# Seven products instead of eight in the second matmul of seven token tiles: operand sums on GpSimd, recombination on VectorE

## Chip, cores, metric

One core of one Trainium2 chip. The metric is the device time of one execution in microseconds (us); medians of several executions are given with their lowest and highest. Ratios are the mean time of one kernel's runs over the mean time of the other kernel's runs of the same rounds on the same chip, so they are not quite the ratio of the medians that are quoted beside them.

The engines' names in the profile are: PE = TensorE matmuls, PEld = TensorE weight loads, DVE = VectorE, ACT = ScalarE, POOL = GpSimd, SP = SyncE, SPq = the queue in which SyncE issues transfers. "L320" is line 320 of the kernel that was profiled. The changed kernel's first lines are one line longer, so L319 of the kernel before is L320 of the changed one. In an experiment, lines below an inserted edit move on: L395 of the changed kernel is L399 in e1 and L401 in e2.

## The reference

```python
# q, k, v: [8 batches, 8 heads, 576 positions, 64]
scores = (q @ k.T) / sqrt(64)
ret = scores * Dmat[head]             # causal decay mask gamma ** (i - j)
x = (ret @ v)                         # reordered to [4608 tokens, 512]
h = x @ w_in                          # 512 -> 2048
g = h * cos(h)
out = g @ w_out                       # 2048 -> 512, float32
```

The attention part is small. The two matmuls by `w_in` and `w_out` make most of the TensorE work.

## The kernel before

The kernel goes through the tokens in ten tiles, of 512, 256, 256 and then seven times 512 tokens; n counts them from 0, so "tile n=3" is the first of the last seven. For each tile it runs the first matmul (`mm1`, eight blocks of 1024 PSUM columns), takes the cosine on ScalarE, multiplies on VectorE into the bfloat16 tile `gT` (this multiplication is called the gate product below), and runs the second matmul (`mm2`). The attention work of the next tile's token groups (128 tokens each) is put between the matmuls of `mm2`, so that TensorE always has something to do:

```python
widths = [512, 256, 256] + [512] * 7
...
def mm1(n, et, c0, w, bank, inside={}):
    ...                                   # 8 matmuls 128x512 into one double bank: a, b or m
    nc.scalar.activation(cosh, ps, ACTF.Sin, bias=half_pi, scale=1.0)
    nc.vector.tensor_mul(gT[:, et : et + m, c0 : c0 + w], ps, cosh)

def mm2(n, tsi, et, c0=0, c1=DM):         # called 64 times in a tile of 512 tokens
    ...
    nc.tensor.matmul(ps, lhsT=gT[:, et, tsi * P : (tsi + 1) * P],
                     rhs=w_out_sb[:, et, c0:c1], start=(et == 0), stop=(et == ET - 1))
    if et == ET - 1:
        nc.scalar.copy(ot, ps)
        nc.sync.dma_start(out[...], ot)
        feed(s)                           # load, prepare and transpose later token groups
```

GpSimd prepares each token group. It scales q and k to bfloat16 and casts v (`prep`):

```python
nc.gpsimd.tensor_tensor(out=qks[:, 0], in0=fq, in1=tq, op=ALU.mult)
nc.gpsimd.tensor_tensor(out=qks[:, 1], in0=fk, in1=tk, op=ALU.mult)
nc.gpsimd.tensor_copy(vb, fv)
```

SyncE issues loads, stores and the transposes of `qks` in one queue, in program order, so a transpose that waits for GpSimd holds up the loads behind it. In the profile of the kernel before, transposes wait for GpSimd 15 times, 20.8 us in all, at most 2.7 us; one that begins at 66.13 us is released by GpSimd at 68.57 (3.46 us with its own issuing), and the load behind it begins at 69.63.

VectorE, besides `gT`, multiplies the masks into the scores (`ret`, out of PSUM banks a and b) and adds up the running attention states (`s`, out of bank st, then copied to bfloat16 `sb`). PSUM has double banks a, b and m, and single banks n and st.

## Time and profile before

In the rounds with the changed kernel, five executions had a median of 308.29 us (307.87 to 310.25). The first three of them alone had 310.21 us (308.17 to 310.25).

From the page of the kernel before: the span and the busy times, then three rows of the 40 equal slices of the span (a digit is the busy share in tenths), then the chain that ended last, by engine and by line (cut off at the end of the excerpt).

```profile
span 304.4 us, 5826 instructions
PE 295.5 (97%) x2411; PEld 169.2 (56%) x2441; DVE 172.9 (57%) x215; ACT 128.2 (42%) x145; POOL 101.1 (33%) x127
...
POOL 2780076445346355444536253415330000000000
PEclk9999999999999999999999999999999999999999
DMA  8999999999989999999999999389923600020012
...
PE 92%; DMA 5%; issue 1%; SPq 1%; DVE 0%; POOL 0%; ACT 0%; ACTq 0%
```

TensorE is the limit: it is busy for 97% of the span, is 92% of the chain, and its granted clock shows as 9 in every slice (0.999 in the mean). GpSimd is idle for two thirds, VectorE for over 40%. But the DMA row is full for the first 60% of the span: GpSimd is idle because it waits for loads. One line of the groups of instructions shows it (busy us and mean ns of one; then the idle time before them and what ended it):

```profile
L136 POOL TENSOR_TENSOR qks<-fq,gq 128x512 bf16<-128x512 f32 x32 | 33.3, 1042 | 98.0 <-DMA fq<-in_q_dram 95.4
```

I cut traces at the start of each tile's `mm1` and call the stretch from one start to the next the tile's period. Here are tiles n=2, 3 and 5 of the kernel before, with the busy times, the granted TensorE clock (PEclk), the busy share of the DMA engines and the rate:

```profile
core 0: us, PE busy (x) PEld busy (x) DVE busy (x) ACT busy (x) POOL busy (x), PEclk, DMA share, GB/s
67.50:83.94 16.44, 16.22 (x163) 11.19 (x165) 9.28 (x13) 6.54 (x7) 8.08 (x9) 1.00 1.21 206
83.94:117.04 33.10, 32.73 (x342) 23.22 (x344) 23.90 (x32) 14.20 (x15) 16.73 (x19) 1.00 1.08 213
...
148.83:180.19 31.36, 30.99 (x238) 15.74 (x240) 20.00 (x25) 13.27 (x14) 14.70 (x17) 1.00 1.23 221
```

TensorE is busy for 99% of each of these periods. This trace is of one of the kernel's quicker executions. A kernel with the same order of work (experiment e4) was traced at 308.46 us, with a span of 306.6 us. In it one transpose came late in tile n=2, TensorE waited 2.3 us for it, and the period was 18.7 instead of 16.4 us. So where the traces' spans are compared below, up to about 2 us in tile n=2 may be such a difference and not the change. The comparison of medians doesn't have this problem to the same degree.

### The profile page before, as it was taken

What the parts mean: (1) busy time and instruction counts of PE and PEld (TensorE: products, weight loads), DVE (VectorE), ACT (ScalarE), POOL (GpSimd) and SP (SyncE); (2) the same over time, 40 slices, a digit from 0 to 9 for tenths busy, and PEclk for the clock granted to TensorE, in tenths of its full rate; (3) what the DMA queues carried; (4) which work ended last, traced back from release to release, by engine and by line L of the source; (5) the groups of instructions that cost most, each with busy time, mean ns of one, the idle gap of its engine ahead of it and who ended that gap; (6) DMA issues with size and microseconds to landing.
All of it is one profiled execution on the core that took longest, in us unless ns stands there. A gap on an engine that the chain in (4) does not pass through costs nothing.

```text
span 304.4 us, 5826 instructions
## 1 busy us (share of the span) xinstructions
PE 295.5 (97%) x2411; PEld 169.2 (56%) x2441; DVE 172.9 (57%) x215; ACT 128.2 (42%) x145; POOL 101.1 (33%) x127
## 2 busy tenths in 40 slices
PE   8899999999999999999999999999999999999995
PEld 3578647758588554445544554455445544554444
DVE  5677514665687665774875566646765557504700
ACT  2656333515256224532364236422652255226511
POOL 2780076445346355444536253415330000000000
PEclk9999999999999999999999999999999999999999
DMA  8999999999989999999999999389923600020012
GB/s 208 202 209 207 208 219 194 220 228 203 209 181 207 220 216 248 228 221 195 223 242 223 187 263 196 49 196 210 254 35 86 89 34 2 34 71 34 0 71 69
DMA packets 150810, 50.19 MB, mean 165 GB/s; under 512 B 140800, under 2 KB 146304, under 8 KB 150784
## 3 DMA queue, kind: packets, MB, share of 16 engines
q1 hardware_dynamic: 146560, 45.63, 79.6%
q0 software_dynamic: 4224, 4.19, 8.4%
q8 instruction: 19, 0.31, 0.5%
q14 instruction: 7, 0.06, 0.1%
HBM read 36.70 MB, written 9.44 MB: 152 GB/s over the span
## 4 chain that ended last, share of the span: by engine, by line
PE 92%; DMA 5%; issue 1%; SPq 1%; DVE 0%; POOL 0%; ACT 0%; ACTq 0%
PE h L319 41%; PE o L336 40%; PE ov L292 3%; PE sc L179 3%; DMA w_in_sb<-in_moe_w_in_dram 2%; DMA fk<-in_k_dram 2%; PE ov L279 2%; PE st L238 1%; SPq L111 1%; PE st L208 0%; DVE xT L304 0%; POOL qks L137 0%; SPq L381 0%; PE tr L157 0%; ACT ot L345 0%
## 5 line engine op out<-in xcount | busy, mean ns | idle before, releaser
L336 PE MATMUL o<-w_out_sb,gT 128*128 128x512 bf16 (+2 forms) x586 | 126.2, 367 | 2.5 <-issue 2.2
L319 PE MATMUL h<-xT,w_in_sb 128*128 128x512 bf16 (+2 forms) x826 | 127.1, 313 | 0.7 <-DMA w_in_sb<-in_moe_w_in_dram 0.2
L328 DVE TENSOR_TENSOR gT<-h,cosh 128x1024 bf16<-128x1024 f32 x72 | 88.2, 1225 | 54.4 <-ACT cosh L327 54.3
L319 PEld LDWEIGHTS <-w_in_sb 128*128 128x128 bf16 x832 | 75.9, 98 | 50.4 <-issue 0.4
L327 ACT ACTIVATE cosh<-h,half_pi 128x1024 f32<-128x1024 f32 x72 | 80.2, 1113 | 51.3 <-PE h L319 51.3
L336 PEld LDWEIGHTS <-gT 128*128 128x128 bf16 x608 | 56.3, 98 | 62.0 <-issue 0.2
L136 POOL TENSOR_TENSOR qks<-fq,gq 128x512 bf16<-128x512 f32 x32 | 33.3, 1042 | 98.0 <-DMA fq<-in_q_dram 95.4
L345 ACT COPY ot<-o 128x512 f32<-128x512 f32 (+2 forms) x38 | 21.4, 563 | 86.4 <-PE o L336 86.3
L137 POOL TENSOR_TENSOR qks<-fk,gk 128x512 bf16<-128x512 f32 x35 | 36.5, 1043 | 16.2 <-DMA fk<-in_k_dram 14.4
L188 DVE TENSOR_TENSOR ret<-sc,tri 128x1024 bf16<-128x1024 f32 x32 | 38.0, 1218 | 4.1 <-PE sc L179 4.0
L304 ACT CAST xT<-ov 128x1024 bf16<-128x1024 f32 (+1 forms) x18 | 16.5, 917 | 21.4 <-PE ov L292 21.2
L143 POOL CAST vb<-fv 128x512 bf16<-128x512 f32 x32 | 19.6, 612 | 6.9 <-DMA fv<-in_v_dram 5.5
L261 DVE TENSOR_TENSOR s<-st,s 128x256 f32<-128x256 f32 x18 | 7.6, 424 | 24.3 <-PE st L238 24.0
L252 DVE CAST sb<-s 64x256 bf16<-64x256 f32 x48 | 19.2, 401 | 0.7
L292 PE MATMUL ov<-ret,vb 128*64 128x128 bf16 x288 | 12.0, 222 | 0.0
L217 DVE TENSOR_TENSOR sb<-st,diag 128x512 bf16<-128x512 f32 x8 | 5.5, 686 | 11.4 <-PE st L208 10.6
L259 DVE COPY s<-st 128x256 f32<-128x256 f32 x6 | 2.5, 424 | 15.8 <-PE st L238 15.8
L179 PEld LDWEIGHTS <-qkT 64*128 64x128 bf16 x288 | 8.1, 94 | 5.0 <-ACT qkT L162 2.3
L279 PEld LDWEIGHTS <-sb 128*128 128x128 bf16 x128 | 8.4, 98 | 3.8
L179 PE MATMUL sc<-qkT 64*128 64x128 bf16 x256 | 10.3, 217 | 0.0
L292 PEld LDWEIGHTS <-vb 128*64 128x64 bf16 x288 | 8.7, 109 | 2.0
L279 PE MATMUL ov<-qkT,sb 128*128 128x128 bf16 (+1 forms) x116 | 8.8, 215 | 0.1
(53 smaller groups left out, 76.3 us busy)
## 6 DMA issues: line engine op xcount, KB each, us to landing
out_dram<-ot SPq DMA_DIRECT2D x35, 256.0 KB, 4.2
fk<-in_k_dram SPq DMA_DIRECT2D x32, 256.0 KB, 4.8
fv<-in_v_dram SPq DMA_DIRECT2D x32, 256.0 KB, 5.0
fq<-in_q_dram SPq DMA_DIRECT2D x28, 256.0 KB, 4.1
w_in_sb<-in_moe_w_in_dram POOLq DMA_DIRECT2D x4, 512.0 KB, 8.6
w_out_sb<-in_moe_w_out_dram POOLq DMA_DIRECT2D x4, 512.0 KB, 15.9
fq<-in_q_dram SPq DMA_DIRECT2D x2, 512.0 KB, 4.4
fq<-in_q_dram SPq DMA_DIRECT2D x8, 128.0 KB, 4.2
```

The costliest lines, as they stand in the source:

```text
L136: nc.gpsimd.tensor_tensor(out=qks[:, 0], in0=fq, in1=tq, op=ALU.mult)
L137: (nc.vector if g == 3 else nc.gpsimd).tensor_tensor(out=qks[:, 1], in0=fk, in1=tk, op=ALU.mult)
L143: nc.gpsimd.tensor_copy(vb, fv)
L179: nc.tensor.matmul(ps[:, he, hg, :], lhsT=qkT[d0 : d0 + D, HG + hg, :], rhs=qT[d0 : d0 + D, hg, :], start=True, stop=True,)
L188: nc.vector.tensor_tensor(out=ret.rearrange("p a b i -> p (a b) i"), in0=ps.rearrange("p a b i -> p (a b) i"), in1=mask.unsqueeze(1).to_br ...
L279: nc.tensor.matmul(ps[:, x, hg, :n], lhsT=sb[:, hg, :], rhs=qT[:, hg, :n], start=(hg == 0), stop=False, skip_group_check=True,)
L292: nc.tensor.matmul(ps[he * D : he * D + D, x, hg, :], lhsT=vb[:, 2 * hg + he, :], rhs=ret[:, he, hg, :], start=(g % PER == 0 and hg == 0), ...
L319: nc.tensor.matmul(ps[:, j, :], lhsT=w_in_sb[:, dg, (et + j) * P : (et + j + 1) * P], rhs=xT[:, dg, c0 : c0 + w], start=(dg == 0), stop=(d ...
L327: nc.scalar.activation(cosh, ps, ACTF.Sin, bias=half_pi, scale=1.0)
L328: nc.vector.tensor_mul(gT[:, et : et + m, c0 : c0 + w], ps, cosh)
L336: nc.tensor.matmul(ps, lhsT=gT[:, et, tsi * P : (tsi + 1) * P], rhs=w_out_sb[:, et, c0:c1], start=(et == 0), stop=(et == ET - 1),)
L345: nc.scalar.copy(ot, ps)
```

## The change

The intent is to save TensorE time with Strassen's method. The second matmul of a 512-token tile is seen as a 2 by 2 product: gT in four quarters (two halves of the tokens by two halves of the inner dimension), `w_out` in four quarters. Instead of eight products of quarters, seven are made, of 16 matmuls of 128x256 each, so 112 matmuls of 256 columns replace 64 of 512. To pay for this, five sums of quarters of gT are needed per tile (2048 elements per partition each, bfloat16), made in two halves. One of them goes to VectorE (two in tile n=3), the others to GpSimd. So that a first half of the sums can be made after block 3, `mm1` takes blocks of the two halves of the inner dimension in turn from tile n=4 on. The weight sums are made once, on VectorE, in tiles n=2 and n=3. VectorE recombines the products out of PSUM by six operations per tile.

The core of the diff (cut; indices of quarters left out):

```diff
+    def g_sum(n, x, e0, e1):              # operand sum of product x, inner blocks e0..e1
+        ...
+        (nc.vector if x == 5 or (n, x) == (S7, 1) else nc.gpsimd).tensor_tensor(
+            out=tiles["gs", n, x][:, e0:e1], in0=i0, in1=i1, op=op_
+        )
+    def sums_after(n, i):                 # after block i of mm1
+        if n == S7:                       # S7 = 3, the first of the seven tiles
+            if i < 4:
+                w_sums(3 + i % 2, i // 2 * 4, i // 2 * 4 + 4)
+            ...                           # gT sums after blocks 6 and 7
+        elif i in (3, 7):
+            for x in (5, 2, 1, 7, 6):
+                g_sum(n, x, i - 3, i + 1)
+    def mm2_seven(n, at):
+        for x in (3, 4, 5, 2, 1, 7, 6):
+            for u in at.get(x, []):       # attention work in front of products 4, 5 and 1
+                u()
+            product(n, x)                 # 16 matmuls 128x256; banks n and st in turn
+            if x == 3:
+                nc.scalar.copy(u22, tiles["o", 3])
+            elif x == 4:
+                nc.vector.tensor_tensor(out=u22, in0=tiles["o", 4], in1=u22, op=ALU.add)
+            elif x == 5:
+                nc.scalar.copy(c12, tiles["o", 3])
+                nc.vector.tensor_tensor(out=u11, in0=u22, in1=tiles["o", 3], op=ALU.subtract)
+                store(c12, 0, 1, s0)      # a store, then feed(), as in mm2
+            ...                           # products 2, 1, 7, 6 likewise
+    def unit7(g, more=True):
+        copy = states([g + 1, g + 2], "b")()   # the states move from bank st into bank b
+        attn_out([g, g + 1], "m", nc.scalar.copy)
+        if more:
+            scores2(g + 2)
+        copy(nc.scalar.copy)              # state copies move from VectorE to ScalarE
...
+            if n == 2 and i < 3:
+                for e in (0, 4):
+                    w_sums((1, 6, 7)[i], e, e + 4)
```

Some buffers are given up to make room: five load buffers instead of six, one gT instead of two, two cosine tiles instead of three, two xT instead of three. The output buffers become four kinds of two. In the last seven tiles, `feed` prepares only groups whose loads were issued at an earlier call. The last output of the kernel, which was stored in smaller pieces before, is now one store of 256 KB.

More of the change, by code (lines that the diff above doesn't have):

```diff
@@ L59 @@
     first = ctx.enter_context(tc.tile_pool(name="first", bufs=1))
-    ld = ctx.enter_context(tc.tile_pool(name="ld", bufs=6))
+    ld = ctx.enter_context(tc.tile_pool(name="ld", bufs=5))
     nat = ctx.enter_context(tc.tile_pool(name="nat", bufs=8))
@@ L64 @@
     stp = ctx.enter_context(tc.tile_pool(name="stp", bufs=2))
-    gp = ctx.enter_context(tc.tile_pool(name="gp", bufs=2))
-    cosp = ctx.enter_context(tc.tile_pool(name="cosp", bufs=3))
-    op = ctx.enter_context(tc.tile_pool(name="op", bufs=4))
-    xp = ctx.enter_context(tc.tile_pool(name="xp", bufs=3))
+    gp = ctx.enter_context(tc.tile_pool(name="gp", bufs=1))
+    sump = ctx.enter_context(tc.tile_pool(name="sump", bufs=1))
+    cosp = ctx.enter_context(tc.tile_pool(name="cosp", bufs=2))
+    op = ctx.enter_context(tc.tile_pool(name="op", bufs=2))
+    xp = ctx.enter_context(tc.tile_pool(name="xp", bufs=2))
     psum = ctx.enter_context(tc.tile_pool(name="psum", bufs=1, space=bass.MemoryType.PSUM))
@@ L223, in state, with states @@
         tiles["sb", g + 1] = sb
-    def states(gs):
+    def states(gs, bank="st"):
         gs = [g for g in gs if g < NG and g % PER != PER - 1]
         if not gs:
-            return lambda: (lambda: None)
-        ps = psum.tile([P, len(gs), HG, D], F32, tag="st", name="st")
+            return lambda: (lambda *_: None)
+        ps = psum.tile([P, len(gs), HG, D], F32, tag=bank, name="st")
         for x, g in enumerate(gs):
@@ L245, in states, with copy @@
                     )
-        def copy():
+        def copy(run=nc.vector.tensor_copy):
             for g in gs:
@@ L251, in copy @@
                     r = slice(he * D, he * D + D)
-                    nc.vector.tensor_copy(sb[r, :, r], s[r])
+                    run(sb[r, :, r], s[r])
                 tiles["sb", g + 1] = sb
@@ L328, in mm1, with mm2 @@
         nc.vector.tensor_mul(gT[:, et : et + m, c0 : c0 + w], ps, cosh)
-    def mm2(n, tsi, et, c0=0, c1=DM):
+    def mm2(n, tsi, et):
         gT = tiles["g", n]
         if et == 0:
-            bank = {0: "nmnm", 1: "nm", 2: "mn"}.get(n, "mnan")[tsi] if c0 == 0 else "ba"[c0 % DM // P % 2]
-            tiles["o", tsi] = psum.tile([P, c1 - c0], F32, tag=bank, name="o")
+            bank = {0: "nmnm", 1: "nm", 2: "mn"}[n][tsi]
+            tiles["o", tsi] = psum.tile([P, DM], F32, tag=bank, name="o")
         ps = tiles["o", tsi]
@@ L338, in mm2 @@
             lhsT=gT[:, et, tsi * P : (tsi + 1) * P],
-            rhs=w_out_sb[:, et, c0:c1],
+            rhs=w_out_sb[:, et, :],
             start=(et == 0),
@@ L343, in mm2, with w_quarter @@
         if et == ET - 1:
-            ot = op.tile([P, c1 - c0], F32, tag="o", name="ot")
+            s = starts[n] // P + tsi
+            ot = op.tile([P, DM], F32, tag="oabcd"[1 + s % 4], name="ot")
             nc.scalar.copy(ot, ps)
-            s = starts[n] // P + tsi
-            nc.sync.dma_start(out[s * P : (s + 1) * P, c0:c1], ot)
+            nc.sync.dma_start(out[s * P : (s + 1) * P, :], ot)
             feed(s)
+    E2 = ET // 2
+    N2 = DM // 2
+    S7 = 3
+    w_sum = {}
+    def w_quarter(r, c):
+        return w_out_sb[:, r * E2 : (r + 1) * E2, c * N2 : (c + 1) * N2]
@@ new lines, in w_sums @@
+    def w_sums(x, e0, e1):
+        a, b, op_ = {
+            3: ((0, 1), (1, 1), ALU.subtract),
+            4: ((1, 0), (0, 0), ALU.subtract),
+            1: ((0, 0), (1, 1), ALU.add),
+            6: ((0, 0), (0, 1), ALU.add),
+            7: ((1, 0), (1, 1), ALU.add),
+        }[x]
+        if x in (3, 4):
+            w_sum[x] = w_quarter(*a)
+        elif x not in w_sum:
+            pool, tag = {1: (consts, "ws1"), 6: (first, "qs4"), 7: (first, "qT4")}[x]
+            w_sum[x] = pool.tile([P, E2, N2], BF16, tag=tag, name=f"ws{x}")
+        nc.vector.tensor_tensor(
+            out=w_sum[x][:, e0:e1],
+            in0=w_quarter(*a)[:, e0:e1],
+            in1=w_quarter(*b)[:, e0:e1],
+            op=op_,
+        )
@@ new lines, in g_sum @@
+    def g_sum(n, x, e0, e1):
+        gT = tiles["g", n]
+        a, b, op_ = {
+            5: ((0, 0), (0, 1), ALU.add),
+            2: ((1, 0), (1, 1), ALU.add),
+            1: ((0, 0), (1, 1), ALU.add),
+            7: ((0, 1), (1, 1), ALU.subtract),
+            6: ((1, 0), (0, 0), ALU.subtract),
+        }[x]
+        if ("gs", n, x) not in tiles:
+            tiles["gs", n, x] = sump.tile([P, E2, 256], BF16, tag=f"gs{x}", name=f"gs{x}")
+        i0, i1 = (
+            gT[:, k * E2 + e0 : k * E2 + e1, r * 256 : (r + 1) * 256] for r, k in (a, b)
+        )
+        (nc.vector if x == 5 or (n, x) == (S7, 1) else nc.gpsimd).tensor_tensor(
+            out=tiles["gs", n, x][:, e0:e1], in0=i0, in1=i1, op=op_
+        )
@@ new lines, in sums_after, with product @@
+    def sums_after(n, i):
+        if n == S7:
+            if i < 4:
+                w_sums(3 + i % 2, i // 2 * 4, i // 2 * 4 + 4)
+            if i == 6:
+                g_sum(n, 5, 0, 4)
+                g_sum(n, 2, 0, 4)
+            elif i == 7:
+                for x, e in ((5, 4), (2, 4), (1, 0), (7, 0), (6, 0)):
+                    g_sum(n, x, e, E2)
+        elif i in (3, 7):
+            for x in (5, 2, 1, 7, 6):
+                g_sum(n, x, i - 3, i + 1)
+    def product(n, x):
+        gT = tiles["g", n]
+        if x in (3, 4, 1, 7):
+            ps = psum.tile([P, 2, N2], F32, tag={3: "n", 4: "st", 1: "n", 7: "st"}[x], name="o")
+            tiles["o", x] = ps
+        else:
+            ps = tiles["o", {5: 3, 2: 4, 6: 1}[x]]
+        lhs = {3: gT[:, :E2, :256], 4: gT[:, E2:, 256:]}.get(x)
+        if lhs is None:
+            lhs = tiles["gs", n, x]
+        rhs = {5: w_quarter(1, 1), 2: w_quarter(0, 0)}.get(x)
+        if rhs is None:
+            rhs = w_sum[x]
+        for e in range(E2):
+            for j in range(2):
+                nc.tensor.matmul(
+                    ps[:, j],
+                    lhsT=lhs[:, e, j * P : (j + 1) * P],
+                    rhs=rhs[:, e, :],
+                    start=(x in (3, 4, 1, 7) and e == j == 0),
+                    stop=(e == E2 - 1 and j == 1),
+                    skip_group_check=True,
+                )
@@ new lines, in mm2_seven, with new, store @@
+    def mm2_seven(n, at):
+        s0 = starts[n] // P
+        def new(tag):
+            return op.tile([P, 2, N2], F32, tag=tag, name="ot")
+        def store(t, r, c, s):
+            r0 = starts[n] + r * 256
+            nc.sync.dma_start(
+                out[r0 : r0 + 256, c * N2 : (c + 1) * N2].rearrange("(j p) c -> p j c", p=P), t
+            )
+            feed(s)
+        for x in (3, 4, 5, 2, 1, 7, 6):
[3 more added lines that the diff above has]
+            if x == 3:
+                u22 = new("a")
+                nc.scalar.copy(u22, tiles["o", 3])
+            elif x == 4:
+                nc.vector.tensor_tensor(out=u22, in0=tiles["o", 4], in1=u22, op=ALU.add)
+            elif x == 5:
+                c12, u11 = new("c"), new("b")
+                nc.scalar.copy(c12, tiles["o", 3])
+                nc.vector.tensor_tensor(out=u11, in0=u22, in1=tiles["o", 3], op=ALU.subtract)
+                store(c12, 0, 1, s0)
+            elif x == 2:
+                c21 = new("d")
+                nc.scalar.copy(c21, tiles["o", 4])
+                nc.vector.tensor_tensor(out=u22, in0=u22, in1=tiles["o", 4], op=ALU.subtract)
+                store(c21, 1, 0, s0 + 1)
+            elif x == 1:
+                nc.vector.tensor_tensor(out=u11, in0=tiles["o", 1], in1=u11, op=ALU.add)
+            elif x == 7:
+                nc.vector.tensor_tensor(out=u11, in0=tiles["o", 7], in1=u11, op=ALU.add)
+                store(u11, 0, 0, s0 + 2)
+            elif x == 6:
+                nc.vector.tensor_tensor(out=u22, in0=tiles["o", 1], in1=u22, op=ALU.add)
+                store(u22, 1, 1, s0 + 3)
@@ L355, in feed @@
         before = loaded
+        late_from = starts[S7] // P
         while True:
-            while prepared < min(loaded, NG, 2 * s + 7, s + 11):
+            while prepared < min(before if s >= late_from else loaded, NG, 2 * s + 7, s + 11):
                 prep(prepared)
@@ L517 @@
         else:
-            blocks = [(et, 0, w) for et in range(0, ET, 1024 // w)]
+            m = 1024 // w
+            blocks = [(et, 0, w) for et in range(0, ET, m)]
+            if n > S7:
+                blocks = [(e + k * E2, 0, w) for e in range(0, E2, m) for k in range(2)]
         banks = {0: "abmabmab", 1: "bmba", 2: "bmab", 3: "mamabmab"}.get(n, "abmabmab")
@@ L529 @@
                 late.pop()()
+            if n == 2 and i < 3:
+                for e in (0, 4):
+                    w_sums((1, 6, 7)[i], e, e + 4)
+            if n >= S7:
+                sums_after(n, i)
         g = starts[n] // P + w // P
@@ L545 @@
             late += [lambda: unit(g + 2, "b", False)]
-        elif n + 1 < len(widths):
-            todo = [
-                (20, lambda: unit(g, "m")),
-                (52, lambda: unit(g + 2, "m", n > 3)),
-            ]
-            if n in (3, 4):
-                todo[0] = (25, lambda: unit(g, "m"))
-                todo.append((12, lambda: scores2(g)))
-        else:
-            todo = []
-        todo.sort(key=lambda u: u[0])
-        order, cols = [], [(0, DM)]
-        for tsi in range(w // P):
-            if (n + 1, tsi + 1) == (len(widths), w // P):
-                cols = [(0, DM // 2), (DM // 2, 3 * DM // 4), (3 * DM // 4, DM)]
-            order += [(tsi, et, c0, c1) for c0, c1 in cols for et in range(ET)]
+        else:
+            at = {}
+            if n + 1 < len(widths):
+                at = {5: [lambda: unit7(g)], 1: [lambda: unit7(g + 2, n > S7)]}
+                if n in (3, 4):
+                    at[4] = [lambda: scores2(g)]
+            mm2_seven(n, at)
+            continue
+        todo.sort(key=lambda u: u[0])
+        order = [(tsi, et) for tsi in range(w // P) for et in range(ET)]
         if n == 0:
             part = 3 * ET // 4
-            order[: 2 * ET] = [
-                (tsi, et, 0, DM)
-                for tsi, et in [(t, e) for e in range(part) for t in range(2)]
-                + [(t, e) for t in range(2) for e in range(part, ET)]
+            order[: 2 * ET] = [(t, e) for e in range(part) for t in range(2)] + [
+                (t, e) for t in range(2) for e in range(part, ET)
             ]
-        for i, (tsi, et, c0, c1) in enumerate(order):
+        for i, (tsi, et) in enumerate(order):
             while todo and todo[0][0] <= i:
                 todo.pop(0)[1]()
-            mm2(n, tsi, et, c0, c1)
+            mm2(n, tsi, et)
         assert not todo
```

## The prediction

> **What bounds it now.** TensorE: the page has it busy 97% of a 304.4 us span, and the chain of waits is 92% TensorE (first matmul L319 41%, second L336 40%). VectorE is 57% busy, GpSimd 33%. But the slice table shows DMA at 90% or more until about 220 us, and the SyncE timeline lags: the output tile finished near 84 us is stored at 112 us. So loads arrive late, and GpSimd mostly waits for them.
>
> **Credit.** Timeline: 64 matmuls of 512 columns take 13.8 us (215.8 ns each); 96 of 256 columns take 10.49 us (109.3 ns). A tile's second matmul falls from 64x215.8=13.8 to 112x109.3=12.2 us, 1.6 us less; seven tiles about 11 us, all on the chain.
>
> **Cost.**
> 1. Weight sums on VectorE in the 256-token tile (six of 1024 bf16, estimated 0.69 us each from its 128x512 float32 op, beside gate products of 1.22 us and a block every 1.75 us): second matmul waits about 2 us.
> 2. GpSimd sums: its 512-element product takes 1.04 us, so 1024 elements about 2.1 us, eight per tile: 16.8 us beside four token groups' preparation (2.7 us each). [...]
> 3. GpSimd's queue is in order. In the first Strassen tile the sums stand behind the preparation of group 17, whose loads let it end only at 111.3 us. TensorE reaches the product S2 at about 109 us, gets its second half at 115.5 us, and waits again for the last sum (124 us): about 7.5 us lost.
> 4. Then a loop: sums, preparation, transpose on the SyncE queue (which waits for that preparation), load behind it (4 us to landing), the preparation two groups on. Transpose issue to end of such a preparation took 8.5 us; so four preparations stretch from 10.8 to about 15 to 16 us. With 16.8 us of sums GpSimd needs 32 to 33 us a tile; TensorE needs 29.8. Tiles 4 to 7 lose 2 to 3.5 us each, tile 8 none.
> 5. Last tile, without attention work between products: 1 to 2 us. Tail: 256 KB after a VectorE add instead of 64 KB: 1 us.
> 6. VectorE's recombination (six of 0.69 us) and ScalarE's copies fit in idle time.
>
> Sum: -11 +2 +7.5 +10 +1.5 +1: about +10 us. The GpSimd duration decides: at 1.8 us per sum it would be +4.
>
> **Prediction: 319 us, 8 in 10 between 307 and 328.** Faster by over 2%: 0.12; within 2%: 0.28; slower by over 2%: 0.60.
>
> **What would show it.** 256-column matmuls of the products at 109 ns; GpSimd busy near 220 us; a GpSimd sum at about 2.1 us; TensorE waits released by GpSimd's sums, largest at S2 in tile 3 (about 5 us), then 2 to 4 us in each of tiles 4 to 7, none in tile 8; GpSimd still waiting for loads between sums; SyncE's transposes waiting for GpSimd; second matmul of the 256-token tile waiting for VectorE's gate products.
>
> **What would make it wrong.** bf16 sums much faster on GpSimd than float32 products; loads arriving earlier; or my reading of the queue order: then tiles 3 to 7 lose nothing and the time is near 303. Worse: VectorE's two-input sums and GpSimd slowing each other ([...] VectorE's casts stretch from 1.2 to 2.3 us beside GpSimd), or the long waits lowering TensorE's granted clock.

Two passages are cut from the recorded text. No term of its sum is among them: the terms add up to +11 us, which it rounds to about +10.

## The result and the profile after

The changed kernel takes 322.44 us (322.04 to 324.61, five runs) against 308.29 us (307.87 to 310.25). The ratio is 1.0473, with a 95% interval of 1.0412 to 1.0534: slower. The output is correct.

The page of the changed kernel, the same rows as shown of before:

```profile
span 322.9 us, 6606 instructions
PE 297.4 (92%) x2745; PEld 201.3 (62%) x2745; DVE 210.9 (65%) x242; ACT 139.4 (43%) x176; POOL 218.9 (68%) x179
...
POOL 2760174455443899499956997799769946950793
PEclk9999999999799969999999999999999999999999
DMA  8999999999999994999199908990899160021012
...
PE 46%; POOL 19%; DVE 11%; DMA 10%; SPq 6%; issue 4%; ACT 3%; POOLq 1%; DVEq 0%
```

The chain is no longer TensorE's alone. GpSimd, DMA and SyncE's queue make 35% of it, after 6% before: most of this is the loop of sums, preparations, transposes and loads that the prediction named in its point 4. VectorE makes another 11%, which is not part of that loop. GpSimd's busy time is 218.9 us, against "near 220" predicted. The clock row has a 7 and a 6 where it had only nines. TensorE's own busy time did not fall (297.4 after 295.5), although it has less to do. Its busy time includes slower matmuls where the clock was lower (more on this below).

The groups of sums and of preparations, as shown of before:

```profile
L395 POOL TENSOR_TENSOR gs<-gT 128x1024 bf16<-128x1024 bf16 (+1 forms) x52 | 116.1, 2271 | 20.3 <-DVE gT L329 20.3
L137 POOL TENSOR_TENSOR qks<-fq,gq 128x512 bf16<-128x512 f32 x32 | 35.1, 1098 | 61.4 <-DMA fq<-in_q_dram 59.4
```

The periods of the same three tiles:

```profile
core 0: us, PE busy (x) PEld busy (x) DVE busy (x) ACT busy (x) POOL busy (x), PEclk, DMA share, GB/s
66.95:88.77 21.82, 18.45 (x164) 11.60 (x164) 14.54 (x18) 6.55 (x7) 11.54 (x12) 0.92 1.24 205
88.77:127.45 38.68, 35.18 (x394) 29.65 (x393) 30.26 (x37) 17.32 (x23) 28.11 (x22) 0.91 1.08 189
...
161.03:194.80 33.77, 30.77 (x291) 20.33 (x289) 22.72 (x24) 15.82 (x21) 27.72 (x21) 1.00 0.87 156
```

All periods, and those of four experiments that are told below (us, from the traces' starts of `mm1`; the last tile ends with the span):

| tile n | before | after | e1: no GpSimd sums | e2: no VectorE sums | e11: no sums, other order | e12: both orders |
|---|---|---|---|---|---|---|
| 2 | 16.4 | 21.8 | 19.7 | 19.6 | 16.3 | 20.0 |
| 3 | 33.1 | 38.7 | 38.4 | 39.8 | 32.6 | 39.2 |
| 4 | 31.8 | 33.6 | 33.3 | 32.3 | 31.9 | 34.0 |
| 5 | 31.4 | 33.8 | 31.1 | 34.3 | 30.2 | 31.1 |
| 6 | 31.1 | 32.5 | 30.9 | 31.9 | 30.0 | 30.4 |
| 7 | 31.4 | 32.6 | 31.1 | 32.3 | 30.2 | 31.1 |
| 8 | 30.7 | 30.7 | 29.4 | 29.4 | 29.3 | 30.1 |
| 9 | 31.1 | 32.2 | 30.1 | 31.3 | 30.1 | 32.2 |

Between the two traces the span grew by 18.5 us: 5.4 in tile n=2, 5.6 in n=3, 6.9 in n=4 to 7 together, nothing in n=8, 1.1 in n=9, less 0.6 before tile n=2. By medians it is 14.2 us: the trace of before is of a quick execution, that of the changed kernel of the slowest of its five (324.61 us).

What TensorE waited for in the changed kernel (us in total, times, longest). In the kernel before, the same list holds no wait over 0.6 us except 1.3 us for the first `zeros` and 2.2 us of small "issue" gaps; where those stand, a matmul's record is missing from the trace.

```profile
PE o L430 <- POOL gs L395: 4.9, 6, 1.5
PE st L239 <- DVE ret L189: 4.2, 2, 2.8
PE sc L180 <- DVE s L262: 3.7, 5, 1.2
PE o L337 <- DVE gT L329: 2.2, 2, 1.9
PE sc L180 <- DVE gT L329: 2.0, 3, 1.2
```

The prediction expected waits for GpSimd's sums of about 5 us in tile n=3 and 2 to 4 us in each of n=4 to 7. They make 4.9 us in all: none in n=3 and n=4, 1.4 to 1.5 us in each of n=5 to 7, and 0.5 in n=9. Waits released by VectorE make 13.7 us (the other four lines, and two left out of 0.9 and 0.7 us); 3.4 us of them lie in tile n=2, behind the weight sums. This is where the prediction was most off, so the experiments had to part GpSimd's share from VectorE's.

Two stretches show how VectorE became a limit without being busy for more than 65% of the span. First, tile n=3 in the changed kernel, on VectorE (start, duration, instruction):

```profile
106.17 1.23 DVE L329 TENSOR_TENSOR gT<-h,cosh 128x1024 bf16<-128x1024 f32 x1
107.31 2.77 DVE L395 TENSOR_TENSOR gs<-gT 128x1024 bf16<-128x1024 bf16 x2
110.01 1.21 DVE L189 TENSOR_TENSOR ret<-sc,tri 128x1024 bf16<-128x1024 f32 x1
111.14 1.21 DVE L189 TENSOR_TENSOR ret<-sc,tri_mix 128x1024 bf16<-128x1024 f32 x1
```

On TensorE at the same time (in brackets: idle time before the instruction, and what released it):

```profile
112.50 0.43 PE L239 MATMUL st<-v_odd,qks 128*64 128x64 bf16 x8 [2.80 <-DVE ret L189]
```

And on GpSimd:

```profile
109.28 1.71 POOL L137 TENSOR_TENSOR qks<-fq,gq 128x512 bf16<-128x512 f32 x1 [0.27 <-DMA fq<-in_q_dram]
...
111.94 0.60 POOL L144 CAST vb<-fv 128x512 bf16<-128x512 f32 x1
112.51 4.20 POOL L395 TENSOR_TENSOR gs<-gT 128x1024 bf16<-128x1024 bf16 x2
```

The last gate product ends at 107.4, and two operand sums stand behind it on VectorE, ahead of the two masks. The running states now use bank b, which the second mask has still to read, so TensorE waits 2.80 us. The GpSimd rows show what was predicted there, 1.2 us later: the preparation ends at 112.5 (111.3 predicted) and the sums come after it. Because TensorE was already held up by VectorE until 112.5, it reached the product that needs those sums so late that they were there. The two delays ran beside each other.

Second, the end of tile n=8, where no preparations are left. VectorE's sum takes 2.58 us:

```profile
276.37 2.58 DVE L395 TENSOR_TENSOR gs<-gT 128x1024 bf16<-128x1024 bf16 x1
278.87 0.68 DVE L461 TENSOR_TENSOR ot<-o,ot 128x512 f32<-128x512 f32 x1
279.47 0.86 DVE L262 TENSOR_TENSOR s<-st,s 128x256 f32<-128x256 f32 x2
```

and TensorE waits for the running state behind it, because the second score block reuses bank b:

```profile
280.48 0.40 PE L180 MATMUL sc<-qkT 64*128 64x128 bf16 x8 [1.24 <-DVE s L262]
```

The same place in experiment e1, which has no sums on GpSimd: VectorE's same sum takes 0.69 us, and the state begins 1.1 us after its end (3.1 us after the sum's start in the changed kernel, 1.8 here).

```profile
267.68 0.69 DVE L399 TENSOR_TENSOR gs<-gT 128x1024 bf16<-128x1024 bf16 x1
...
269.44 0.87 DVE L262 TENSOR_TENSOR s<-st,s 128x256 f32<-128x256 f32 x2
```

In the changed kernel's trace, a GpSimd sum ran from 276.27 to 278.40 us, and VectorE's, begun at 276.37, ended 0.54 us after it: the 2.58 us are the rest of that GpSimd sum and most of the operation itself. The same shows at all six operand sums of VectorE that begin while a GpSimd sum runs. They take 0.97 to 2.58 us, each ends 0.54 or 0.55 us after that GpSimd sum, and GpSimd's next one takes 2.58 or 2.59 us, where the median is 2.13. The other six from tile n=4 on take 0.69 us. Two of these began 0.11 us before a GpSimd sum, and that one took 2.57 and 2.58 us. So in this trace the sum that began first kept its time, and the other paid. VectorE's gate products, which read one input from PSUM, keep 1.22 us in the changed kernel.

Waits also cost twice, because the granted clock fell after some of them. The trace of the changed kernel has the clock at 1.00 or at 0.50, and, but for its end, at 0.50 in two stretches, of 3.41 and 6.83 us (columns as in the tables of periods above):

```profile
80.98:84.39 3.41, 3.41 (x9) 1.21 (x8) 1.74 (x2) 0.59 (x1) 1.17 (x2) 0.50 0.96 182
111.70:115.11 3.41, 2.61 (x46) 2.32 (x48) 2.10 (x4) 0.18 (x1) 3.41 (x4) 0.50 1.33 242
```

The second goes on to 118.53. The first came behind waits of TensorE of 1.88 and 1.18 us, which ended at 78.17 and 80.51 us; the second began 2.0 us into the wait of 2.80 us. In the 3.41 us before each of the two falls TensorE was idle for 1.79 and 2.00 us. The length of one wait did not decide it: the 2.3 us of e4's late transpose brought no fall (its run had a mean clock of 1.0), and in e5 a wait of 2.81 us for the same masks, up to 111.70, has no slower matmuls behind it. What decides it is not shown. 3.41 us at half clock cost TensorE 1.7 us of work; the changed kernel's trace has 5.1 us of such a cost, the trace of before none until its last 0.6 us. It is not the main cause of the loss: of the five executions, the one with the highest mean clock (0.995) still took 322.04 us, the two with the lowest (0.984) 322.85 and 324.61.

### The profile page after: what moved, and what is told of

The parts are those of the page before. It is cut to its first block, busy times and chain, and to the rows that moved or that the text cites. A ratio compares the mean times of both kernels' runs of the same rounds, so it can differ in the third digit from the quotient of the medians.

```text
span 322.9 us, 6606 instructions
## 1 busy us (share of the span) xinstructions
PE 297.4 (92%) x2745; PEld 201.3 (62%) x2745; DVE 210.9 (65%) x242; ACT 139.4 (43%) x176; POOL 218.9 (68%) x179
## 4 chain that ended last, share of the span: by engine, by line
PE 46%; POOL 19%; DVE 11%; DMA 10%; SPq 6%; issue 4%; ACT 3%; POOLq 1%; DVEq 0%
PE h L320 21%; POOL gs L395 15%; PE o L430 11%; PE o L337 8%; DVE gT L329 4%; SPq L112 4%; DMA fk<-in_k_dram 4%; DMA fq<-in_q_dram 3%; DMA fv<-in_v_dram 3%; ACT cosh L328 2%; DVE ws L373 2%; PE sc L180 2%; POOL qks L137 2%; POOL qks L138 2%; PE ov L293 2%
## 5 line engine op out<-in xcount | busy, mean ns | idle before, releaser
L395 POOL TENSOR_TENSOR gs<-gT 128x1024 bf16<-128x1024 bf16 (+1 forms) x52 | 116.1, 2271 | 20.3 <-DVE gT L329 20.3
L430 PEld LDWEIGHTS <-gs 128*128 128x128 bf16 x560 | 53.8, 99 | 15.8 <-POOL gs L395 6.9
L430 PE MATMUL o<-ws,gs 128*128 128x256 bf16 x336 | 38.4, 273 | 0.5 <-POOL gs L395 0.5
L337 PE MATMUL o<-w_out_sb,gT 128*128 128x512 bf16 x128 | 32.0, 396 | 2.2 <-DVE gT L329 2.2
L430 PE MATMUL o<-w_out_sb,gs 128*128 128x256 bf16 x224 | 27.8, 281 | 5.2 <-POOL gs L395 4.4
L430 PE MATMUL o<-w_out_sb,gT 128*128 128x256 bf16 x224 | 25.9, 273 | 0.0
L430 PEld LDWEIGHTS <-gT 128*128 128x128 bf16 x224 | 21.7, 98 | 4.0
L337 PEld LDWEIGHTS <-gT 128*128 128x128 bf16 x128 | 12.1, 101 | 16.4 <-issue 2.8
L395 DVE TENSOR_TENSOR gs<-gT 128x1024 bf16<-128x1024 bf16 (+1 forms) x15 | 18.3, 1228 | 0.4
L253 ACT CAST sb<-s 64x256 bf16<-64x256 f32 x40 | 16.1, 403 | 0.6
L347 ACT COPY ot<-o 128x512 f32<-128x512 f32 x8 | 4.7, 588 | 21.6 <-PE o L337 21.6
```

What stands on the lines that cost most here:

```text
L395: (nc.vector if x == 5 or (n, x) == (S7, 1) else nc.gpsimd).tensor_tensor(out=tiles["gs", n, x][:, e0:e1], in0=i0, in1=i1, op=op_)
L430: nc.tensor.matmul(ps[:, j], lhsT=lhs[:, e, j * P : (j + 1) * P], rhs=rhs[:, e, :], start=(x in (3, 4, 1, 7) and e == j == 0), stop=(e == ...
```

## The experiments

The expectations use letters. A is the theory of the prediction: GpSimd's sums, their duration and their place in its in-order queue, carry the loss. B lays it on VectorE: its added work and the order of its queue. C lays it on the buffers that were given up, D on the products themselves, their order and recombination, so that the credit isn't there. Kernels marked WRONG compute a wrong output. They leave sums out and give the product a quarter of gT or of the weights, so that TensorE's work, the stores and the recombination are as in the changed kernel. Executions over 1.5% slower than the fastest of the same kernel are left out of the means. "Before" in the same rounds had medians of 307.6 to 308.2 us. The changed kernel itself was not timed again in these rounds.

| experiment | output | median us (lowest to highest) | ratio to before |
|---|---|---|---|
| changed kernel | right | 322.44 (322.04 to 324.61) | 1.0473 |
| e1 no GpSimd sums | WRONG | 312.72 (312.25 to 314.7) | 1.0131 |
| e2 no VectorE sums | WRONG | 318.96 (318.15 to 320.92) | 1.0327 |
| e3 no sums | WRONG | 306.36 (304.62 to 306.58) | 0.9901 |
| e4 buffers only | right | 308.56 (308.0 to 309.87) | 0.9991 |
| e5 load first | right | 322.69 (321.37 to 324.52) | 1.0457 |
| e6 second sum on VectorE | right | 345.27 (343.48 to 346.13) | 1.1177 |
| e7 all sums on VectorE | right | 352.36 (350.64 to 353.7, three runs) | 1.1474 |
| e8 last two tiles only | right | 316.95 (313.41 to 318.1) | 1.024 |
| e9 last six tiles | right | 318.81 (317.78 to 320.93, three runs) | 1.035 |
| e10 attention first | right | 322.28 (321.99 to 324.37) | 1.0466 |
| e11 no sums, attention first | WRONG | 301.17 (299.57 to 301.92) | 0.9777 |
| e12 load first and attention first | right | 316.73 (316.48 to 317.03) | 1.0304 |

### e1: no sums on GpSimd (WRONG on purpose)

```diff
 # in g_sum
+        if x != 5 and (n, x) != (S7, 1):
+            r, k = a
+            tiles["gs", n, x] = gT[:, k * E2 : (k + 1) * E2, r * 256 : (r + 1) * 256]
+            return
```

> The products S2, S1 (from the second Strassen tile on), S7 and S6 read a quarter of the gate tile in place of a sum; GpSimd forms no sum, everything else stays. Results are wrong on purpose. Theory A (GpSimd's in-order queue of sums and preparation holds TensorE): the 14 us lost come back and most of the 11 us credit shows, 300 to 305 us; no TensorE wait on GpSimd sums, tiles 4 to 7 of about 30 us. Rival B (VectorE's sums and recombination): stays above 315 us. Rival C (smaller buffers): stays above 315 us.

Measured 312.72 us. GpSimd's sums are worth 9.7 us beside VectorE's sums, not all of the loss: 4.4 us above before remain. In the table of periods, tiles n=5 to 7, which took between 32.5 and 33.8 us, fall to about 31, tile n=8 falls to 29.4, and tile n=3 stays at 38.4. So in tiles n=5 to 7 GpSimd's sums are the limit, and in tile n=3 it makes no difference to have none. The result lies between what the two theories expected.

### e2: no sums on VectorE (WRONG on purpose)

```diff
 # in w_sums
+        w_sum[x] = w_quarter(*a)
+        return
 # in g_sum
+        if x == 5 or (n, x) == (S7, 1):
+            r, k = a
+            tiles["gs", n, x] = gT[:, k * E2 : (k + 1) * E2, r * 256 : (r + 1) * 256]
+            return
```

> VectorE forms no operand sum and no weight sum, the products read quarters; GpSimd's sums stay. Wrong on purpose. A: only the waits for VectorE go, mainly the 3.4 us in the 256-token tile and some of the 2.8 us in the first Strassen tile, but GpSimd's loop of 32 to 34 us a tile remains: 316 to 320 us. B: 305 to 310 us.

Measured 318.96 us, in the range of A. VectorE's sums are worth 3.5 us. Again tile n=3 did not fall (39.8 us). With VectorE's sums gone, TensorE's waits for GpSimd's sums appear there, as the prediction had them (but smaller, 2.08 us for the first half and 1.03 for the second instead of about 5; the first is shown). The matmuls behind them were slower: eight of 256 columns took 1.05 us at 113.82 and 1.89 us at 115.89, sixteen took 2.82 us at 120.25 and 1.92 us at 109.82. Summed up to 122.9 us, such differences make about 2.8 us (an estimate from these rows) of the 6.7 that this tile lost; the mean granted clock of the run was 0.977:

```profile
113.82 1.05 PE L436 MATMUL o<-w_out_sb,gs 128*128 128x256 bf16 x8 [2.08 <-POOL gs L401]
```

A batch of eight GpSimd sums took 16.70 us here, 17.18 us in the changed kernel in a middle tile and 17.61 us in tile n=8. So GpSimd loses 0.5 to 0.9 us per batch beside VectorE's sums. Tile n=8 fell to 29.4 us, as in e1. So the 1.3 us that the changed kernel loses in tile n=8 need both sums at once, and neither engine's alone costs anything there.

### e3: no sums at all (WRONG on purpose)

Both edits together.

> No sums at all, neither of operands nor of weights: seven products and their recombination alone. Wrong on purpose. If the narrower matmuls give their 11 us (A and B agree): 297 to 301 us. Rival D (256-column matmuls, their extra weight loads and the recombination eat the credit): 306 us or more.

Measured 306.36 us, 1.9 us below before by medians, where A had expected 297 to 301. So D is partly right: with all sums free, the seven products as they are ordered here give little. TensorE's waits in this kernel, as totals:

```profile
PE sc L180 <- DVE s L262: 2.5, 4, 0.7
PE sc L180 <- DMA qkT<-qks: 1.8, 1, 1.8
```

The first is the running state on VectorE, which stands behind a recombination step and holds bank b. It is not part of the arithmetic, only of the order. The second is the late transpose that e4 has too. Tile n=3 took 34.1 us, and its first 32 matmuls 4.91 us (3.66 in the kernel before); the granted clock was 0.90 from 82 to 99 us (1.00 in the kernel before).

### e4: the kernel before with the changed kernel's buffers

```diff
-    ld = ctx.enter_context(tc.tile_pool(name="ld", bufs=6))
+    ld = ctx.enter_context(tc.tile_pool(name="ld", bufs=5))
-    gp ... bufs=2 / cosp ... bufs=3 / op ... bufs=4 / xp ... bufs=3
+    gp ... bufs=1 / cosp ... bufs=2 / op ... bufs=2 of each of four tags / xp ... bufs=2
```

> The kernel before with the changed kernel's buffer counts: load 5 for 6, gate tile 1 for 2, cosine 2 for 3, attention output 2 for 3, output tiles four tags of two. Right results. A: within 0.7% of before, since TensorE finishes a tile before the next gate tile is written. C: 3% or more slower.

Measured 308.56 us, ratio 0.9991 (0.9929 to 1.0052). The buffers cost nothing in the old order of work. C falls.

### e11: e3, and the attention's running sums ahead of recombination

This was run later. It leaves all sums out, as e3, and puts two recombination steps behind the running sums of the attention on VectorE:

```diff
             elif x == 4:
-                nc.vector.tensor_tensor(out=u22, in0=tiles["o", 4], in1=u22, op=ALU.add)
+                behind.append(lambda ...: nc.vector.tensor_tensor(out=u22, in0=o, in1=u22, op=ALU.add))
             elif x == 2: ...              # likewise
 # in unit7, after the states' matmuls and sums; and ahead of the next product
+        flush()                            # now issue what is in behind
```

> The run without any sums, with the same reordering. Wrong on purpose. There the waits for the running sums are 2.5 us of what the credit lacks: 303 to 305 us beside 306.4 us, if the order on VectorE is part of where the credit went; 306 us or more if only the order of matmul shapes and the clock took it.

Measured 301.17 us (ratio 0.9777), better than expected. The trace is of the quickest execution (299.57 us). After the kernel's start, no wait of TensorE in it is longer than 0.4 us; the longest group:

```profile
PE sc L180 <- DVE gT L329: 0.8, 2, 0.4
```

So the full credit of the seven products, with free sums, is about 7 us (4 to 10 by the interval of the ratio, 0.9688 to 0.9867), where the prediction counted 11. In a middle tile (n=5 to 7) it is 1.1 us instead of 1.6. The matmuls are as counted: the profile has the last three products, 48 matmuls of 256 columns, start to start in 5.25 us, 109.3 ns each. Where the other half microsecond of the tile goes can be read from the starts of matmuls in n=5: the seven products take 12.43 us with the edges between them (12.24 counted), and the attention matmuls 3.99 us, against about 3.7 before. Why the same attention matmuls take longer there is not shown. The tail's cost is also inside the 7 us.

### e5: loads ahead of transposes

```diff
 # in feed
-            if N_PE_T <= transposed < min(prepared, s + 11) and (
+            if s >= late_from and loaded < min(NG, 2 * s + 8, s + 13):
+                load(loaded)
+                loaded += 1
+            elif N_PE_T <= transposed < min(prepared, s + 11) and (
```

> In the Strassen tiles the loads of a token group are issued ahead of the transpose that waits for GpSimd, not behind it; nothing else changes and results are right. A, in its loop form (sums, preparation, transpose, load behind it, preparation): GpSimd's preparation phase between two tiles' sums falls from about 15 us to about 12.5 us, its cycle from 32.5 us to about 30 us, and tiles 5 to 7 lose 1 to 2.5 us less each: 316 to 319 us beside 322.4. If the loop is no limit and only the sums' own length counts, or VectorE: 321 us or more.

Measured 322.69 us: no gain, a miss. The intended part came true. GpSimd is no longer late: before the batches of sums of tiles n=5 to 7 it now waits for gT, 5.2, 3.7 and 3.1 us. Those tiles take 32.4, 31.8 and 32.4 us instead of 33.8, 32.5 and 32.6. But tile n=4 went from 33.6 to 36.2 us, and over the whole kernel TensorE's waits for the running state rose from 3.7 and 0.9 us to 5.8 and 1.3. In tile n=4 the batch now starts at 136.0 instead of 140.4 us, and with it the moment shifts at which VectorE's second operand sum meets a sum of GpSimd. VectorE in tile n=4 of e5:

```profile
142.82 2.57 DVE L395 TENSOR_TENSOR gs<-gT 128x1024 bf16<-128x1024 bf16 x1
```

The masks come behind it, and TensorE, in the same kernel, waits for them:

```profile
147.80 0.42 PE L239 MATMUL st<-vb,qks 128*64 128x64 bf16 x8 [2.71 <-DVE ret L189]
148.16 1.03 PE L280 MATMUL ov<-qkT,sb 128*128 128x128 bf16 x8
```

In the changed kernel the same sum took 1.30 us and TensorE waited 1.44 us. In both traces GpSimd's batch was running. There its sum ended 0.75 us after VectorE's began (144.62 and 143.87); here VectorE's took 2.57 us, as long as the two of the changed kernel that began 0.1 us after a GpSimd sum (2.58). So the difference in this tile is by all signs one of phase, not of GpSimd being early as such. After the 2.71 us the clock fell too (0.95 over the tile, 1.00 in the changed kernel): eight matmuls that took 0.62 us in the changed kernel's same place take 1.03 us.

### e10: the attention's running sums first on VectorE

The edit of e11, with all sums in place.

> On VectorE the running attention sums, which release the bank of the second score block, come ahead of two recombination steps, not behind them. Right results, all work kept. TensorE's waits for those running sums (4.6 us in the profile) should fall to about 2 us. If they are truly on the path: 319 to 321 us; if the time is set by the sums alone: 322 us or more.

Measured 322.28 us: no gain either. The waits for the running state fell from 3.7 and 0.9 us to 0.6 and 0.5, and the waits for GpSimd's sums rose from 4.9 to 8.0 us (longest 2.7). TensorE came earlier to the sums and waited for GpSimd instead.

### e12: both orders

The edits of e5 and e10 together.

> Both reorderings at once: loads ahead of the transpose, and the running attention sums ahead of the recombination. Each alone left the time at 322 us: with the loads first GpSimd waited for gate products and TensorE for the running sums; with the sums first TensorE waited 8 us for GpSimd. If these are two limits that hide each other: tiles 5 to 7 fall from 32.5 to 33.8 us to 30.5 to 31.5 us and the time to 314 to 318 us. If either is no limit at all and something else sets the time: 321 us or more.

Measured 316.73 us, as expected: 5.7 us less by medians, where each edit alone gave nothing (0.2 more and 0.2 less). TensorE's waits for GpSimd's sums are down to 0.7 us and those for the running state to 1.5 and 0.6 us. Tiles n=5 to 7 take 31.1, 30.4 and 31.1 us, as in e1 without any GpSimd sums. This is the clearest sign that two limits of about the same size stood in parallel: taking away either shows nothing, taking away both shows both. What remains over before is in tiles n=2 and 3 (3.5 and 6.1 us over the trace of before), n=4 (2.2) and n=9 (1.1).

### e6 and e7: more sums on VectorE

If GpSimd is the limit and VectorE is busy for 65%, moving sums over should help.

```diff
 # e6
-        (nc.vector if x == 5 or (n, x) == (S7, 1) else nc.gpsimd).tensor_tensor(
+        (nc.vector if x in (5, 2) or (n, x) == (S7, 1) else nc.gpsimd).tensor_tensor(
 # e7
+        nc.vector.tensor_tensor(
```

> A fourth Strassen operand sum, that of S2, goes from GpSimd to VectorE (VectorE two, GpSimd three in a tile). Right results. A: GpSimd's cycle falls by 2 x 2.14 us and S2 no longer waits for it, so tiles 5 to 7 fall to about 31 us: 314 to 319 us, with the first Strassen tile still near 38 us, where VectorE is late too. B (VectorE decides): slower than 322 us.

> All five operand sums on VectorE, GpSimd only prepares. Right results. Without GpSimd beside it a sum of 1024 takes VectorE about 0.7 us, so 5.5 us more a tile for VectorE. A: GpSimd's loop is gone and the time is near that of the run without GpSimd's sums (312.7 us) plus what VectorE's longer queue costs: 312 to 318 us. B: 325 us or more.

Measured 345.27 and 352.36 us (a fourth run of e7, 356.55 us, was slow): the largest misses. In e6 one more sum on VectorE costs 23 us. VectorE's sums have a mean of 1557 ns there, beside GpSimd's, against 832 in e1 without them. In e7 no sum is left on GpSimd, and the mean (814 ns) is not the matter: the sums come as a row of five between two gate products. The waits of TensorE in e7:

```profile
PE h L320 <- DVE gT L329: 17.9, 8, 3.7
PE st L239 <- DVE ret L189: 11.0, 2, 8.0
```

A row of five sums takes 3.1 to 5.2 us, while a block of `mm1` comes every 1.75 us and there are three double banks. TensorE stops in `mm1` (first line), which the changed kernel doesn't have. B's expectation held in both.

### e8 and e9: Strassen on fewer tiles

If the cost is the loop of preparations, the last tiles, which have none, should gain. e8 uses seven products in tiles n=8 and 9 only, with two sums on VectorE and three on GpSimd; e9 in all but n=3.

```diff
-    S7 = 3
+    S7 = 8        # e9: 4; the weight sums move to tiles S7 - 1 and S7
...
-        (nc.vector if x == 5 or (n, x) == (S7, 1) else nc.gpsimd).tensor_tensor(
+        (nc.vector if x in (5, 2) else nc.gpsimd).tensor_tensor(        # e8 only
+        elif n < S7:
+            ...                                   # the old order for earlier tiles
```

> Strassen only in the last two tiles, where no token group is left to prepare; VectorE forms two of the five sums, GpSimd three; the other tiles as before, the buffers as in the changed kernel. Right results. A: GpSimd has nothing else to do, so neither tile waits for it: the eighth tile falls from 30.7 to about 29.5 us and the last from 31.0 to about 30.3 us: 305.5 to 307.5 us, just ahead of before. Rivals (VectorE, bank and recombination costs): 309 us or more.

> Strassen from the tile after, so in the last six tiles; the weight sums move one tile later and are spread over six and five blocks. Right results. The first Strassen tile is where VectorE's sums, GpSimd's late sums and a fallen clock met (38.7 us beside 33.1 us before). If that comes from its being the first with full loads pending (group 17 in front of the sums, as predicted), the loss goes and the kernel comes to 311 to 314 us. If it comes from VectorE doing weight sums, operand sums and masks in one stretch, the loss moves into the next tile in part: 314 to 319 us.

e8 measured 316.95 us, ratio 1.024 (1.0183 to 1.0297); 305.5 to 307.5 was expected. Tiles n=8 and 9 took 33.9 and 33.2 us, each more than before. VectorE and GpSimd got in each other's way. VectorE in tile n=8:

```profile
254.18 3.22 DVE L395 TENSOR_TENSOR gs<-gT 128x1024 bf16<-128x1024 bf16 x2
```

GpSimd beside it:

```profile
254.22 7.70 POOL L395 TENSOR_TENSOR gs<-gT 128x1024 bf16<-128x1024 bf16 x3 [28.86 <-DVE gT L329]
```

Three GpSimd sums took 7.70 us (6.3 at the 2.09 us of e2), a pair of VectorE's 3.22 us (1.4 at 0.69 us each), and TensorE waited 1.7 us in `mm1` of each tile for gate products behind such a pair, and 1.9 us for the running state behind the second pair of tile n=8. So the loss isn't only in the preparation loop. Its times came in two clusters, two at 313.4 and four at 316.4 to 318.1 us, and the profile is of the lower. The granted clock parts them: 0.999 in the lower cluster, 0.989 to 0.995 in the upper. Why the clock fell in some executions only is open.

e9 measured 317.78, 318.81 and 320.93 us in three runs, ratio 1.035 (1.0245 to 1.0455); a fourth, with 378.37 us at a granted clock of 0.754, was slow and is left out. Its profile fell on that slow run and is not used. Leaving out tile n=3, which lost 5.6 us, saves 3.6 us by medians; the weight sums and the first operand sums move to tiles n=3 and 4. This fits the second of the two readings, that the tile that comes first pays, whichever it is; without a fast profile it is not shown.

### A version that beats both?

None was found. The best right kernels are the one before and e4 (308.3 and 308.6 us), and the most that seven products with free sums brought in any run is e11's 301.2 us, 2.3%, of a kernel with wrong output.

## Why the prediction was right or wrong

The total (319 us, 307 to 328) and the direction held at 322.44 us. The sum behind it held less well. One way through the runs adds up to the whole loss, with medians: from before to e11, the products with free sums and a good order, -7.1 us; from e11 to e3, the change's own order on VectorE, +5.2; from e3 to e2, GpSimd's sums, +12.6; from e2 to the changed kernel, VectorE's sums, +3.5. Together +14.2 us. Another way through e1 gives VectorE's sums 6.4 and GpSimd's 9.7 us. The terms are not additive because the two engines hide and block each other. Point by point:

**Credit, -11 us: mis-sized.** The products' matmuls ran at 109.3 ns, as predicted, beside 215.8 ns for 512 columns in the kernel before (64 in 13.81 us). But the credit was -7.1 us in e11 and only -1.9 us in e3, in the order that the change has.

**Step 1, weight sums, +2 us: too small, by how much depends on the comparison.** Tile n=2 lost 5.4 us against the trace of before, 3.1 against e4's and 2.2 against e2's, which has no weight sums; the last two have the late transpose. The six weight sums took 1.04 us each in the mean, not 0.69 (four beside GpSimd's preparations 1.02 to 1.53 us, the other two 0.68), TensorE waited 0.31, 1.88 and 1.18 us for the gate products behind them, and its clock was then at 0.50 for 3.41 us (0.92 over the tile).

**Step 2, GpSimd's sums: right.** 2.15 us per sum and 17.18 us per batch, against 2.1 and 16.8. Where VectorE makes no sums (e2) it was 2.09 us. A float32 product of 512 elements takes 1.04 us, so here bfloat16 sums were no faster for each element.

**Step 3, first Strassen tile, +7.5 us: the size was near, the wait was another.** The tile lost 5.6 us net, against 5.9 predicted (7.5 less the credit of 1.6). GpSimd's queue was late as predicted, to within 1.2 us. But TensorE's wait was for VectorE's masks (2.80 us), and the wait for the product S2 that should be about 5 us did not come. The granted clock was at 0.50 from 111.70 to 118.53 us, which costs 3.4 us of TensorE's work, as much as all waits of the tile (3.4 us); the prediction's sum had no such term. e1 and e2 show that taking away either engine's sums leaves this tile at 38.4 or 39.8 us, and e3 without both has 34.1. GpSimd's delay was real (e2 shows its waits) and hidden.

**Step 4, the loop of sums and preparations: right in mechanism, right in cycle.** 32 to 33 us were predicted; the starts of the batches in tiles n=4 to 7 lie 34.5, 32.5 and 32.6 us apart, and the periods of n=4 to 7 are 33.6, 33.8, 32.5 and 32.6 us. e1 brings n=5 to 7 back to 31 us. A preparation phase between two batches shows the wait for loads of which the prediction spoke:

```profile
140.41 17.18 POOL L395 TENSOR_TENSOR gs<-gT 128x1024 bf16<-128x1024 bf16 x8
...
172.00 1.04 POOL L137 TENSOR_TENSOR qks<-fq,gq 128x512 bf16<-128x512 f32 x1 [4.41 <-DMA fq<-in_q_dram]
...
174.92 2.13 POOL L395 TENSOR_TENSOR gs<-gT 128x1024 bf16<-128x1024 bf16 x1
```

The waits of TensorE that it should cause, 2 to 4 us for sums in each tile, were 1.4 to 1.5 us in n=5 to 7 and none in n=4, because VectorE had delayed TensorE before it came to the sums. e10 took that delay away, and the waits for the sums rose to 8.0 us. Tile n=8 has no wait for GpSimd, as predicted, but lost its credit to the blocked VectorE sum instead.

**Step 5, last tile and tail, 1 to 2 and 1 us: right.** Tile n=9 grew by 1.1 us, against 0.9 predicted (1.5 + 1 less 1.6).

**Step 6, "VectorE's recombination (six of 0.69 us) and ScalarE's copies fit in idle time": this is the step that failed.** The recombination steps do take 0.68 to 0.69 us each. VectorE's share of the span rose from 57 to 65%, which looks like room. But it is in the order of the queue that they cost: a recombination step or an operand sum ahead of a mask or a running state holds bank b, and TensorE waits. Of the change's VectorE order, 5.2 us show from e11 to e3 by medians. (e3's trace has the late transpose of tile n=2 and e11's hardly; in the other tiles the two traces differ by 4.4 us, 1.25 us of slower matmuls at the start of n=3 included.) In the changed kernel VectorE releases 13.7 us of TensorE's waits. Part of these is not step 6's: the weight sums' 3.4 us, and what VectorE's operand sums hold up, for which the sum of the prediction had no term at all. For the same reason e6 and e7 went the wrong way by 23 and 30 us.

**What was named as a risk** came true in both parts: VectorE's sums and GpSimd's blocked each other, and the granted clock fell after waits (5.1 us of TensorE's work in the trace). I had put both under "worse", outside of the sum, and they made up for a loss in GpSimd's waits that was smaller than predicted. Of +7.5 and +10 us for GpSimd, e1 and e2 show 9.7 to 12.6. So the total was right partly because errors cancelled.

**Open:** how much of the 14.2 us is the clock's (3.41 us at half clock cost TensorE 1.7 us of work, but may hide in a wait for another engine); why it fell behind waits of 1.88 and 1.18 us and not behind e4's of 2.3 or e5's of 2.81 us; what makes the transpose of tile n=2 late in some executions; and why the attention matmuls between products take a quarter of a microsecond more per tile in e11.

## What to carry to other kernels

Before giving an engine more work because its busy share leaves room, write down its queue order around each operation that TensorE waits for: here recombination steps of 0.69 us in front of the running states made 5.2 us of the kernel's time (e11 to e3, by medians). Before splitting sums between VectorE and GpSimd, count on what was seen here, that a VectorE sum of 0.69 us takes up to 2.58 us beside GpSimd's of 2.13; if both must run, their stretches could alternate or GpSimd's instructions be made short, neither of which was tried here. When removing one suspected cost moves nothing, try it together with its rival before dropping either: in e5, e10 and e12 two parallel limits hid each other.
